# RWKV attention, Fourier mix and MLP on one core: weights requested later, masks from two-input VectorE operations, sums and state carry of two batches moved to VectorE, a new order

## The chip, the cores and the metric

The kernel runs on one core of a Trainium2 chip. Times are device microseconds (us), from launch to end; the span of a profile is from its first to its last instruction and is a little shorter. Five engines work side by side, each through its own list of instructions: TensorE (PE; its weight loads are shown as PEld), ScalarE (ACT), VectorE (DVE), GpSimd (POOL) and SyncE (SP), which issues most DMAs. They meet at semaphores.

## The reference

Inputs are r, k, v, w of 4 batches x 8 heads x 768 steps x 48, u of 8 x 48, and the two MLP weights. The attention is a recurrence over time, and its output goes through a Fourier mix, a normalization and an MLP:

```
state = 0
for t in range(S):
    cur = einsum('bhd,bhe->bhde', u * k[t], v[t])
    y[t] = einsum('bhd,bhde->bhe', r[t], state + cur)
    state = w[t][..., None] * state + einsum('bhd,bhe->bhde', k[t], v[t])
x = y as (batch, 768, 384)
u = x + real(fft(fft(x, axis=1), axis=2))
un = (u - mean(u)) / sqrt(var(u) + 1e-6)
out = u + relu(un @ w_ch1) @ w_ch2        # 384 -> 1536 -> 384
```

## The kernel before

**Attention.** Each batch is cut into 6 chunks of 128 steps; chunk n is step c = n mod 6 of batch n // 6 (24 chunks). The function attention does one: SP loads w, k, r, v (192 KB each, 7 buffers of each, L434). ACT takes ln of w (L586). PE forms two sums of it over time with two matmuls of 384 columns, one with the strict mask MSK (L588, "cumE") and one with the negated mask NLE (L592, "cumI"), in two PSUM banks, tce and tci, and the chunk's total beside the second (L599, "tot", or with one mask matmul more "totm", L603). ACT takes exp of both (L594; L609 and L611 in batch 0, or the one exp2 of L613 later). DVE multiplies r into the first (rh, L628); k is multiplied into the second by DVE in batch 0 (L632) and by POOL later (kh, L636). POOL forms r*k*u, DVE sums it (dc, L620), POOL scales v by it (vtd, L623). PE transposes rh and kh (L644, L650), ACT evicts both (rtb, ktb, L653, L655), PE forms the scores (amat, L663), DVE masks and evicts them in two halves (ah, L668). PE forms the chunk's state (L680), adding the old state with an identity matmul of 384 columns (L678); DVE scales it by the decay, in batch 0 with one operation (stm, L687), later with two halves (st, L694). PE forms y (L704, L708). The term of u and v is added in batch 0 by an fp32 matmul ("diag", L716, then ACT copies x, L720) and later by a DVE addition (x, L722). DVE and POOL fold x for the Fourier transform (fold_d, L737: columns of x plus and minus their mirror image, helper line L399).

**Mix and MLP.** The function mix does one batch: PE matmuls of the folded x with the cosine and sine tables CS and SS (L764, "mmh"), ACT evicts (hcs, L772), POOL reverses (hcr, L774), matmuls with DTM and DTP (L785, "mm2"), DVE adds x (uf, L787) and takes mean and variance (L791, L793: bn_stats, bn_aggr), ACT normalizes (un, L796), PE transposes (L802), ACT evicts (unt, L807). Then two halves of three blocks of 128 rows each: 12 m1 blocks of 3 matmuls with W1 (L826), whose relu is done by ACT (L835) or, for two of twelve, DVE (L831), and 3 m2 blocks of 12 matmuls with W2 (L845), which DVE scales and adds to u (osb, L850) and SP stores (L854).

**Start.** POOL makes index rows with iota; DVE makes four masks from them with tensor_scalar (masks, L457 to L460); DVE and ACT make a quarter of the tables with sine (tables, L484); DVE mirrors them (mirrors, L506); ACT copies halves of them with sign +1 and -1 (tables_end, L526); PE picks rows (L549) and ACT evicts them as DTM and DTP (L553, L555). POOL requests the weights (L560, L562) once the k load of chunk 5 has landed; the w load of chunk 7, and so all of SP's list behind it, waits for W1 (L436). Twenty warm-up steps of two matmuls (L887) are spread over the first part.

**Order.** Every operation has a number, in the order in which the program text creates it. The list ORDER, written out at the top, gives all 1511 of them in one sequence; each engine's list is its share of that sequence, in that order, and it never leaves it: an operation that waits holds up all behind it on its engine. BANKS gives the PSUM bank of each tile in turn. The function op derives who waits for whom from what each operation reads and writes, and arrange adds the waits for a bank's last users. Priorities such as KW and the ready0 of the warm-up steps have no effect on the chip except through ORDER.

Of the kernel before, what the change touches and what calls it, by code (L numbers as in the profile page):

```python
# [12 lines left out]
    70, 0, 3, 7, 8, 9, 6, 1, 11, 10, 2, 4, 71, 72, 46, 73, 42, 44, 45, 43, 41, 5, 12, 34,  # L13
    37, 74, 40, 19, 105, 25, 1491, 20, 26, 75, 106, 21, 13, 23, 32, 22, 14, 24, 27, 107, 1492, 15, 29, 28,
    17, 16, 108, 76, 84, 30, 18, 88, 1493, 137, 38, 85, 31, 138, 35, 36, 86, 1494, 109, 49, 139, 77, 50, 110,
    111, 33, 87, 112, 78, 79, 140, 81, 80, 113, 121, 1495, 116, 82, 89, 123, 114, 169, 141, 91, 39, 48, 115, 93,
    142, 170, 122, 117, 1496, 83, 144, 143, 90, 145, 124, 125, 171, 47, 92, 146, 148, 153, 98, 1497, 94, 99, 172, 155,
    120, 95, 118, 149, 51, 130, 97, 147, 201, 173, 1498, 154, 126, 119, 175, 177, 202, 131, 157, 174, 127, 96, 176, 156,
    203, 53, 1499, 129, 180, 152, 100, 101, 158, 128, 204, 54, 181, 162, 150, 102, 159, 185, 178, 233, 132, 151, 205, 182,
    1500, 184, 187, 163, 234, 206, 104, 133, 179, 189, 161, 183, 208, 271, 235, 186, 1501, 134, 207, 52, 212, 160, 209, 188,  # L20
    210, 236, 194, 217, 190, 164, 55, 1502, 213, 211, 216, 195, 429, 191, 237, 165, 218, 136, 193, 430, 1503, 166, 261, 219,
    192, 239, 238, 221, 431, 272, 103, 220, 240, 242, 214, 196, 241, 279, 432, 247, 197, 246, 135, 262, 222, 249, 167, 280,
    56, 58, 281, 248, 198, 226, 215, 251, 282, 250, 227, 433, 223, 168, 263, 252, 224, 264, 265, 200, 283, 273, 225, 253,
    243, 435, 255, 1504, 228, 199, 229, 59, 244, 266, 254, 64, 230, 245, 256, 231, 65, 257, 232, 57, 284, 60, 267, 258,
    434, 274, 66, 275, 259, 61, 436, 260, 285, 268, 63, 286, 287, 276, 269, 288, 289, 290, 62, 67, 270, 458, 277, 444,
    459, 439, 291, 293, 302, 460, 446, 68, 322, 461, 294, 69, 303, 440, 304, 448, 295, 1505, 305, 443, 340, 437, 278, 441,
    311, 312, 438, 313, 292, 306, 1506, 1507, 445, 314, 341, 1508, 307, 315, 308, 1509, 442, 296, 447, 309, 449, 331, 316, 297,
    332, 1510, 317, 450, 298, 299, 323, 451, 324, 453, 310, 318, 333, 325, 300, 319, 342, 455, 301, 334, 320, 363, 321, 343,
    351, 326, 364, 487, 353, 462, 454, 344, 352, 359, 488, 354, 327, 367, 345, 335, 328, 365, 452, 346, 489, 357, 468, 336,
    368, 456, 358, 373, 490, 457, 337, 469, 369, 374, 349, 355, 516, 360, 491, 470, 464, 466, 371, 467, 517, 471, 492, 356,  # L30
    361, 494, 474, 493, 518, 372, 375, 502, 366, 362, 380, 472, 497, 519, 501, 463, 495, 350, 338, 465, 551, 381, 498, 496,
    473, 376, 370, 552, 503, 339, 499, 475, 520, 347, 482, 477, 553, 522, 526, 524, 484, 505, 348, 476, 483, 525, 382, 554,
    500, 530, 329, 507, 377, 383, 586, 532, 330, 504, 478, 378, 390, 587, 527, 506, 479, 391, 400, 481, 555, 588, 396, 561,
    528, 557, 511, 480, 397, 589, 559, 565, 402, 562, 401, 560, 521, 783, 485, 403, 567, 392, 563, 523, 590, 394, 512, 784,
    531, 393, 529, 412, 395, 513, 533, 785, 413, 534, 595, 535, 508, 486, 569, 536, 379, 592, 510, 385, 596, 599, 509, 594,
    537, 384, 540, 571, 564, 597, 386, 787, 539, 786, 598, 556, 404, 538, 558, 812, 591, 601, 514, 405, 566, 543, 593, 813,
    541, 568, 793, 814, 544, 603, 570, 408, 515, 605, 789, 815, 546, 791, 600, 572, 409, 414, 573, 797, 841, 794, 816, 398,
    574, 818, 842, 406, 545, 399, 788, 549, 602, 407, 548, 542, 820, 843, 387, 790, 795, 822, 604, 798, 578, 844, 792, 419,
    388, 550, 826, 579, 575, 799, 870, 845, 410, 577, 606, 576, 411, 871, 581, 415, 608, 821, 847, 607, 849, 872, 828, 420,
    850, 625, 817, 873, 609, 547, 855, 584, 800, 819, 585, 610, 421, 802, 905, 580, 633, 634, 874, 635, 636, 611, 807, 416,  # L40
    906, 809, 583, 422, 801, 612, 876, 878, 907, 803, 808, 626, 617, 618, 627, 417, 836, 879, 614, 424, 827, 389, 884, 616,
    837, 628, 629, 804, 582, 908, 630, 909, 829, 613, 637, 615, 638, 631, 639, 640, 619, 838, 886, 641, 620, 940, 621, 831,
    622, 806, 911, 642, 913, 623, 643, 644, 830, 805, 632, 941, 846, 645, 888, 851, 647, 848, 656, 423, 665, 890, 648, 856,
    649, 666, 646, 832, 667, 942, 650, 810, 624, 657, 914, 658, 668, 425, 857, 919, 943, 651, 944, 426, 659, 880, 652, 1137,
    859, 669, 653, 694, 695, 660, 1138, 696, 861, 796, 676, 677, 670, 685, 661, 671, 427, 858, 418, 654, 921, 686, 662, 697,
    687, 672, 865, 811, 655, 428, 881, 663, 673, 698, 678, 833, 664, 679, 923, 860, 1139, 823, 713, 834, 674, 925, 721, 680,
    1140, 852, 675, 709, 714, 824, 1166, 722, 723, 882, 710, 915, 1167, 717, 853, 724, 725, 835, 718, 1168, 949, 711, 688, 726,
    715, 681, 712, 1169, 689, 854, 875, 682, 719, 716, 877, 1147, 727, 1195, 699, 690, 720, 885, 705, 700, 916, 728, 1196, 707,
    691, 701, 887, 708, 950, 862, 1197, 706, 692, 864, 839, 702, 734, 693, 1148, 867, 1141, 866, 739, 703, 863, 825, 953, 735,
    704, 951, 889, 883, 1198, 917, 868, 1224, 683, 840, 736, 1151, 1176, 1225, 869, 684, 1226, 910, 1149, 891, 1170, 1205, 766, 892,  # L50
    912, 740, 920, 1227, 1150, 729, 737, 952, 1259, 893, 894, 744, 895, 1177, 730, 738, 767, 745, 896, 758, 918, 1260, 756, 759,
    1234, 1178, 897, 757, 1261, 746, 1180, 898, 1206, 922, 747, 752, 1262, 924, 748, 899, 1294, 753, 926, 1179, 1207, 749, 741, 928,
    1295, 900, 946, 731, 742, 948, 1296, 927, 945, 955, 764, 947, 732, 929, 743, 1199, 1142, 903, 957, 765, 954, 902, 760, 1144,
    733, 901, 959, 956, 1235, 930, 1201, 932, 761, 931, 1297, 1203, 958, 754, 933, 904, 1209, 1143, 1152, 960, 1208, 1204, 1145, 755,
    971, 979, 762, 1228, 1236, 935, 1146, 750, 962, 763, 980, 1172, 751, 1174, 934, 1154, 1175, 1171, 768, 1153, 961, 1263, 1173, 769,
    1156, 936, 1182, 1181, 1155, 963, 1157, 770, 964, 1238, 939, 1184, 1161, 965, 1183, 1186, 972, 1158, 1211, 1162, 1185, 973, 1163, 773,
    1159, 968, 774, 1160, 966, 1187, 771, 1200, 1190, 1188, 1298, 772, 1164, 970, 775, 1202, 1165, 937, 1273, 987, 1191, 988, 989, 990,
    1237, 991, 1189, 981, 982, 983, 992, 984, 1230, 1232, 985, 938, 1193, 967, 993, 1233, 994, 969, 974, 995, 975, 776, 1307, 996,
    1265, 1240, 976, 1300, 1192, 997, 977, 998, 777, 1213, 1194, 1219, 999, 978, 1001, 1210, 1019, 1215, 1267, 1002, 1269, 1220, 1020, 1268,
    1021, 1221, 1003, 1242, 1022, 1302, 1248, 1270, 1244, 1004, 1229, 778, 1231, 1023, 1275, 1212, 1005, 1010, 1011, 1214, 1024, 1012, 1239, 779,  # L60
    1025, 1000, 1006, 1013, 1277, 1007, 986, 1241, 1271, 1030, 1309, 1279, 1031, 1014, 780, 1243, 1015, 1026, 1303, 1016, 1008, 781, 1048, 1049,
    1028, 1050, 1009, 1017, 782, 1272, 1216, 1051, 1027, 1039, 1217, 1040, 1018, 1032, 1304, 1245, 1029, 1218, 1071, 1059, 1247, 1072, 1073, 1305,
    1060, 1065, 1052, 1074, 1306, 1077, 1246, 1066, 1067, 1033, 1078, 1079, 1053, 1068, 1034, 1061, 1054, 1035, 1063, 1080, 1062, 1311, 1055, 1064,
    1075, 1313, 1069, 1076, 1041, 1088, 1056, 1070, 1036, 1042, 1081, 1043, 1037, 1093, 1038, 1082, 1089, 1044, 1057, 1045, 1094, 1058, 1046, 1095,
    1047, 1264, 1100, 1096, 1266, 1102, 1101, 1097, 1274, 1299, 1118, 1103, 1301, 1276, 1098, 1119, 1308, 1278, 1222, 1114, 1099, 1249, 1090, 1223,
    1115, 1250, 1251, 1091, 1283, 1106, 1252, 1092, 1284, 1280, 1254, 1107, 1285, 1112, 1281, 1310, 1113, 1110, 1258, 1282, 1312, 1083, 1253, 1111,
# [219 lines left out]
def bass_rwkv6_finch__then__fnet_fourier_mix_kernel(  # L286
# [11 lines left out]
    DM = H * D  # L298
# [585 lines left out]
    for i in range(NW):  # L884
        def warm(e):
            for x in range(2):
                ins = e.matmul(ps(tw)[:, 0:384], MSK[:, :], IDW[:, :])  # L887
# [33 lines left out]
```

## Time and profile before

| | |
|---|---|
| median of 5 runs | 203.4 us (200.49 to 205.51) |
| the profiled execution | 203.4 us, span 201.4 us |
| TensorE clock granted | 1.00 |
| MLP matmuls (m1, m2) | 576, 128 x 384 columns |
| DMA | 26.26 MB, loads of 192 KB land 3.8 to 4.0 us after issue (median) |
| SP waits for W1 | 7.6 us, once |

The page of a profile gives, for each engine, busy time and share, then the span in 40 equal slices (digits are tenths busy), the DMA queues, the chain of work that ended last, and the costliest groups. Further views used below: windows (busy time per engine in stretches), the chain in order of time, the timeline, and groups kept apart by shape. In a group's row, "x48 | 31.5, 682 | 4.0 <-PE" means 48 instructions, 31.5 us busy, 682 ns each, 4.0 us of idle time just ahead of them, ended by PE. Instructions of one engine overlap a little, so two in a row start closer together than one lasts.

### The profile page before, as it was taken

The page shows a single profiled execution, that of the slowest core. Times are in us where ns is not written, and L with a number is a line of the kernel's source. Part 1 is how long each engine was busy: PE and PEld are TensorE (multiplying, and loading weights), DVE is VectorE, ACT ScalarE, POOL GpSimd, SP SyncE. Part 2 cuts the span into 40 slices and gives each one's busy share as a digit, 9 for nine tenths or more (in the row PEclk, how much of TensorE's full clock was granted, in tenths as well). Part 3 has the DMA queues.
Part 4 walks back from the last instruction along what each step waited for, and adds up shares of the span by engine and source line. Part 5 has one row for each costly group of instructions (what it writes and reads, how often), then busy time and mean ns, then how long its engine had stood idle before and what let it go on. Part 6 is the DMA issues. An engine that isn't in the chain of part 4 may idle for free.

```text
span 201.4 us, 4633 instructions
## 1 busy us (share of the span) xinstructions
PE 185.7 (92%) x1765; PEld 116.4 (58%) x1765; DVE 154.5 (77%) x340; ACT 144.6 (72%) x332; POOL 119.2 (59%) x148
## 2 busy tenths in 40 slices
PE   2798986996999999999999989999999999999993
PEld 1155653644666676676675656776666566665661
DVE  7889999566846999989989799999557985913123
ACT  5979982667999988689994788598966304795500
POOL 5685892467099898799999889698101653000000
PEclk9999999999999999999999999999999999999999
DMA  5999899999799999997898990111001011200033
GB/s 120 211 206 199 168 184 200 184 184 208 143 211 182 235 203 178 212 213 188 171 180 169 219 238 5 39 42 39 3 0 58 26 39 39 80 1 0 0 108 130
DMA packets 105272, 26.26 MB, mean 130 GB/s; under 512 B 100257, under 2 KB 104866, under 8 KB 105250
## 3 DMA queue, kind: packets, MB, share of 16 engines
q1 hardware_dynamic: 103298, 23.60, 55.3%
q0 software_dynamic: 1952, 2.36, 6.9%
q8 instruction: 14, 0.23, 0.5%
q14 instruction: 8, 0.07, 0.1%
HBM read 23.59 MB, written 4.72 MB: 141 GB/s over the span
## 4 chain that ended last, share of the span: by engine, by line
PE 44%; DVE 19%; SPq 13%; DMA 11%; POOL 6%; ACT 3%; issue 3%; DVEq 0%; POOLq 0%
PE bank L826 15%; PE bank L845 14%; SPq L434 13%; DMA in_v<-in_v_dram 9%; DVE ah L668 4%; POOL rk L399 3%; PE bank L785 3%; DVE xf L399 3%; DVE osb L850 2%; DMA in_r<-in_r_dram 2%; DVE xa L399 2%; PE bank L764 2%; PE bank L663 2%; DVE x L722 2%; DVE st L694 2%
## 5 line engine op out<-in xcount | busy, mean ns | idle before, releaser
L826 PE MATMUL bank<-unt,w 128*128 128x384 bf16 x288 | 54.1, 326 | 0.5 <-ACT unt L807 0.5
L845 PE MATMUL bank<-w,ht 128*128 128x384 bf16 x288 | 54.1, 326 | 0.0
L835 ACT ACTIVATE ht<-bank 128x384 bf16<-128x384 f32 x80 | 37.7, 495 | 15.3 <-PE bank L826 15.1
L826 PEld LDWEIGHTS bank<-unt,w 128*128 128x128 bf16 x288 | 26.1, 97 | 16.8 <-issue 0.8
L845 PEld LDWEIGHTS bank<-w,ht 128*128 128x128 bf16 x288 | 26.6, 98 | 15.6 <-DVE ht L831 0.2
L668 DVE TENSOR_TENSOR ah<-bank,msk 128x512 bf16<-128x512 f32 x48 | 31.5, 682 | 4.0 <-PE bank L663 3.8
L399 POOL TENSOR_TENSOR vtd<-in_v,dc 128x384 f32<-128x384 f32 x24 | 19.9, 833 | 16.8 <-DVE dc L620 15.8
L399 POOL TENSOR_TENSOR rk<-in_r,in_k 128x384 f32<-128x384 f32 x24 | 24.5, 1025 | 4.6 <-DMA in_r<-in_r_dram 4.1
L850 DVE SCALAR_TENSOR_TENSOR osb<-bank,rstd,x 128x384 f32<-128x384 f32 x24 | 14.7, 612 | 14.2 <-PE bank L845 11.4
L399 POOL TENSOR_TENSOR rk<-rk,ub 128x384 f32<-128x384 f32 x24 | 24.2, 1015 | 0.9
L399 POOL TENSOR_TENSOR kh<-in_k,e 128x384 bf16<-128x384 f32 x18 | 19.0, 1058 | 3.8 <-ACT e L613 3.8
L655 ACT ACTIVATE ktb<-bank 128x512 bf16<-128x512 bf16 x24 | 14.5, 610 | 5.2 <-PE bank L650 5.2
L399 POOL TENSOR_TENSOR xd<-x 128x385 f32<-128x385 f32 x9 | 9.0, 1003 | 14.6 <-DVE x L722 14.6
L628 DVE TENSOR_TENSOR rh<-bank,in_r 128x384 bf16<-128x384 f32 x24 | 13.1, 550 | 5.7 <-ACT bank L594 4.2
L413 ACT ACTIVATE un<-x,agg 128x384 bf16<-128x384 f32 x24 | 14.0, 611 | 3.0 <-DVE agg L793 3.0
L787 DVE TENSOR_TENSOR x<-bank,x 128x384 f32<-128x384 f32 x24 | 12.8, 545 | 4.0 <-PE bank L785 3.8
L653 ACT ACTIVATE rtb<-bank 128x512 bf16<-128x512 bf16 x24 | 14.7, 611 | 1.5 <-PE bank L644 1.3
L831 DVE TENSOR_SCALAR ht<-bank 128x384 bf16<-128x384 f32 x16 | 8.7, 549 | 8.8 <-PE bank L826 8.8
L620 DVE TENSOR_REDUCE dc<-rk 128x8 f32<-128x384 f32 x24 | 12.8, 543 | 2.6 <-POOL rk L399 1.9
L887 PE MATMUL bank<-idw,msk 128*128 128x384 bf16 x40 | 11.1, 383 | 3.9 <-DVE idw L403 3.9
L413 ACT ACTIVATE lb<-in_w 128x384 bf16<-128x384 f32 x24 | 12.9, 540 | 2.4 <-PE bank L588 1.9
L413 ACT ACTIVATE vb<-in_v 128x384 bf16<-128x384 f32 x24 | 12.7, 536 | 2.0 <-DMA in_v<-in_v_dram 1.5
(119 smaller groups left out, 380.8 us busy)
## 6 DMA issues: line engine op xcount, KB each, us to landing
in_w<-in_w_dram SPq DMA_DIRECT2D x24, 192.0 KB, 3.8
in_k<-in_k_dram SPq DMA_DIRECT2D x24, 192.0 KB, 4.0
in_r<-in_r_dram SPq DMA_DIRECT2D x24, 192.0 KB, 3.9
in_v<-in_v_dram SPq DMA_DIRECT2D x24, 192.0 KB, 3.9
out_dram<-osb SPq DMA_DIRECT2D x24, 192.0 KB, 2.3
w<-in_moe_w_ch_dram POOLq DMA_DIRECT2D x2, 1152.0 KB, 13.6
ht<-in_u_dram SPq DMA_DIRECT2D x1, 1.5 KB
```

Of the source, the lines that this page charges most:

```text
L399: return shared(lambda e: e.tensor_tensor(out=o, in0=a, in1=b, op=f))
L413: return lambda e: e.activation(o, a, f, **kw)
L434: return e.dma_start(INB[n][i][:, :, :], src[n][b, :, c * CH:(c + 1) * CH, :].rearrange("h t d -> t h d"))
L620: op("dve", "dc", lambda e: e.tensor_reduce(out=dc[:, :], in_=rku[:, :, :], axis=mybir.AxisListType.X, op=ALU.add), r=[("RK", i2)], w=[("D ...
L628: op("dve", "rh", lambda e: e.tensor_tensor(out=rh[:, :, 0:D], in0=ps(tce)[:, 0:DM].rearrange("t (h d) -> t h d", d=D), in1=rt[:, :, :], o ...
L653: op("act", "ev512", lambda e: e.activation(rT[:, :, :].rearrange("p h t -> p (h t)"), psb(trr)[:, 0:512], ACTF.Copy), r=[trr], w=[("RTB", ...
L655: op("act", "ev512", lambda e: e.activation(kT[:, :, :].rearrange("p h t -> p (h t)"), psb(trk)[:, 0:512], ACTF.Copy), r=[trk], w=[("KTB", ...
L668: masked[n] = op("dve", "ah", lambda e, x=x: e.tensor_tensor(out=ah[:, x:H:2, :], in0=ps(ta[x])[:, :].rearrange("p (h t) -> p h t", t=128) ...
L826: ins = e.matmul(ps(t)[:, 0:384], W1[:, m, 128 * j:128 * j + 128], unt[:, m, :], start=(m == 0), stop=(m == NM - 1))
L835: op("act", "ev384", lambda e, j=j, t=t, ht=ht: e.activation(ht[:, j, :], ps(t)[:, 0:384], ACTF.Relu), r=[t], w=[("HT", q % 2, j)])
L845: ins = e.matmul(ps(t)[:, 0:DM], ht[:, j, 128 * x:128 * x + 128], W2[:, j, :], start=(j == 0), stop=(j == NJ - 1))
L850: op("dve", "osb", lambda e, kb=kb, t=t, o=o: e.scalar_tensor_tensor(out=o[:, :], in0=ps(t)[:, 0:DM], scalar=rstd[:, kb:kb + 1], in1=uf[:, ...
```

## The change

- The weight requests no longer wait for k of chunk 5 but for w of chunk 6. In POOL's new list W1 stands behind vtd of chunk 4, W2 behind kh of chunk 6.
- Masks and the small constant rows (MSK, NLE, IDF, IDW, NEGM, SGB, SGS, H5, CP) are made with scalar_tensor_tensor, whose second input is a column of constants KC; the negated identity NIDW is made with the masks. POOL's zero fills now wait for the tables (TG).
- The second and third table halves (UPE) are made by DVE with KC columns in place of ACT; CS and SS rows are one element longer.
- In batches 2 and 3 (chunks 12 to 23, TCD) the second sum isn't a matmul: DVE adds ln w to the first sum in PSUM ("tcd", into the E2 buffer in SBUF), and ACT takes exp of its negative ("expn"). The total stands in the first sum's bank (exp4), so a chunk uses one bank less.
- In the chunks of those batches that have a state before and after (13 to 16 and 19 to 22, SAD) PE doesn't add the old state; DVE does ("sadd", PSUM plus SBUF, into the fp32 buffer SA) and scales in one operation ("sams", two SBUF inputs) in place of the two st halves. Their total is of the kind totm.
- Chunk 5 gets its diagonal term from the DVE addition in place of diag and the ACT copy.
- Warm-up: 13 + 16 steps on a zero tile WZ, filled at the start, in place of 20 on the mask.
- ORDER (1530 operations now) and BANKS are new throughout. In the new lists the row picks and evictions of DTM and DTP stand among the first two or three chunks in place of after chunk 5, and y of chunk 6 stands before the first m1.

```diff
-            chain(op("sp", "load", f, r=["W1"] if b * NC + c == NC + 1 and n == "w" else (), w=[("in", n, i)],
-                     sem="in_%s%d" % (n, i)))
+            o = op("sp", "load", f, r=["W1"] if b * NC + c == NC + 1 and n == "w" else (), w=[("in", n, i)],
+                   sem="in_%s%d" % (n, i))
+            chain(o)
+            loads[b * NC + c, n] = o
...
-        op("dve", "fill1", fill(PM1[:, 0:1], 1.0), w=["PM1a"])
-        op("dve", "fill1", fill(PM1[:, 1:2], -1.0), w=["PM1b"])
+        op("dve", "fill384", fill(WZ[:, :], 0.0), w=["WZ"])
+        for i, x in enumerate((1.0, -1.0, 0.5, -1e4)):
+            op("dve", "fill1", fill(KC[:, i:i + 1], x), w=["KC%d" % i])
...
-        op("dve", "cmp384", ts(IDW[:, :], CI[:, :], 0.0, None, ALU.is_equal), r=["CI"], w=["IDB"])
+        op("dve", "cmps384", stt(IDW[:, :], CI[:, :], 0.0, KC[:, 0:1].to_broadcast([128, 384]), ALU.is_equal, ALU.mult), r=["CI", "KC0"], w=["IDB"])
+        op("dve", "cmps384", stt(NIDW[:, :], CI[:, :], 0.0, KC[:, 1:2].to_broadcast([128, 384]), ALU.is_equal, ALU.mult), r=["CI", "KC1"], w=["NIDW"])
...
-            op(e, kind, fill(o, 0.0), w=w)
+            op(e, kind, fill(o, 0.0), r=[("TG", q) for q in range(3)] if e == "pool" else (), w=w)
...
-        op("dve", "neg384", ts(NIDW[:, :], IDW[:, :], -1.0, None, ALU.mult), r=["IDB"], w=["NIDW"])
...
+    ws, WN = [], ((6, "w"), (6, "w"))
+
     def weights():
-        op("pool", "loadw", lambda e: e.dma_start(W1[:, :, :], moe_w_ch1.rearrange("(q p) n -> p q n", p=128)),
-           r=[("in", "k", 5)], w=["W1"], sem="w1")
...
+        ws.append(op("pool", "loadw", lambda e: e.dma_start(W1[:, :, :], moe_w_ch1.rearrange("(q p) n -> p q n", p=128)),
+           w=["W1"], sem="w1"))
...
-    KHD, DIAG, RKD = range(6), range(6), ()
-    FE, UPE, MST, HCD = ("act", "pool", "pool", "pool"), ("act", "act"), range(NC), ()
+    KHD, DIAG, RKD = range(6), range(5), ()
+    FE, UPE, MST, HCD = ("act", "pool", "pool", "pool"), ("dve", "dve"), range(NC), ()
+    TCD, SAD = range(12, 24), range(12, 24)
...
-        mst = n in MST
+        sad = n in SAD and not first
+        mst = n in MST or sad
+        tcd = n in TCD
...
-        tce, tci = g.tile(pool), g.tile(pool)
+        tce = g.tile(pool)
+        tci = tce if tcd else g.tile(pool)
...
-        if early:
+        if tcd:
+            op("dve", "tcd", lambda e: e.tensor_tensor(
+                out=e2[:, :, :], in0=ps(tce)[:, 0:DM].rearrange("t (h d) -> t h d", d=D), in1=L[:, :, 0:D], op=ALU.add),
+               r=[tce, ("LB", i2)], w=[("E2", i2)])
+            if not last:
+                op("act", "exp4", lambda e: e.activation(E2[i2][:, DM:ne], ps(tce)[:, DM:ne], ACTF.Exp), r=[tce], w=[("WE", i2)])
+            op("act", "exp", lambda e: e.activation(ps(tce)[:, 0:DM], ps(tce)[:, 0:DM], ACTF.Exp), w=[tce])
+            op("act", "expn", lambda e: e.activation(E2[i2][:, 0:DM], E2[i2][:, 0:DM], ACTF.Exp, scale=-1.0), w=[("E2", i2)])
+        elif early:
...
-                if not first:
+                if not first and not sad:
                     e.matmul(ps(tds)[:, 0:DM], IDB[:, :], s_in.rearrange("p h d -> p (h d)"), start=True, stop=False)
...
+            if sad:
+                op("dve", "sadd", lambda e: e.tensor_tensor(
+                    out=SA[:, :, :, :].rearrange("p h x d -> p (h x d)"), in0=ps(tds)[:, 0:DM],
+                    in1=s_in.rearrange("p h d -> p (h d)"), op=ALU.add),
+                   r=[tds, ("ST", (c + 1) % 2, 0), ("ST", (c + 1) % 2, 1)], w=["SA"])
             if mst:
-                op("dve", "stm", lambda e: e.tensor_tensor(
+                op("dve", "sams" if sad else "stm", (shared if sad else lambda f: f)(lambda e: e.tensor_tensor(
...
-    W0, WP, NW = 4.0, 1.6, 20
+    W0, WP, NW = 1.4, 0.65, 13
+    W1T, WP1, NW1 = 10.5, 1.6, 16
...
+    for o, n in zip(ws, WN):
+        o.deps.add(loads[n])
...
-                ins = e.matmul(ps(tw)[:, 0:384], MSK[:, :], IDW[:, :])
+                ins = e.matmul(ps(tw)[:, 0:384], WZ[:, 0:128], WZ[:, :])
```

## The prediction, made before the changed kernel was run

> **What bounds the kernel now.** I read the page first: shares of busy time, then the slices.
>
> ```profile
> span 201.4 us, 4633 instructions
> PE 185.7 (92%) x1765; PEld 116.4 (58%) x1765; DVE 154.5 (77%) x340; ACT 144.6 (72%) x332; POOL 119.2 (59%) x148
> ...
> DVE  7889999566846999989989799999557985913123
> ```
>
> TensorE (PE) leads, VectorE (DVE) is full in slices 14 to 28 and free at the end. Each engine works through its own list in ORDER, so counting a list off against the timeline names every instruction. Four stages follow: until the first m1 matmul of the MLP (50.0), until x of chunk 11 (83.1), until x of chunk 23 (163.1), the rest. The windows:
>
> ```profile
> 0.00:40.00 40.00, 30.89 (x297) 17.64 (x298) 34.96 (x81) 29.85 (x68) 25.57 (x37) 1.00 0.99 184
> 40.00:83.00 43.00, 41.09 (x425) 25.90 (x423) 33.28 (x71) 37.20 (x89) 32.40 (x37) 1.00 0.99 193
> 83.00:125.00 42.00, 40.86 (x425) 26.78 (x424) 38.33 (x83) 34.45 (x80) 39.38 (x45) 1.00 0.85 179
> 125.00:163.00 38.00, 37.74 (x391) 24.83 (x390) 31.74 (x71) 26.33 (x60) 18.14 (x24) 1.00 0.08 28
> 163.00:201.40 38.40, 35.15 (x236) 21.24 (x233) 16.16 (x37) 16.77 (x39) 3.73 (x6) 1.00 0.15 52
> ```
>
> Columns are PE, PEld, DVE, ACT, POOL, granted clock, DMA share, GB/s. A pipelined PE looks busy while it waits, so I count matmul work instead, by start-to-start times: 0.163 us for 384 columns (40 in 6.51 us in the chain), 0.083 for 192, 0.055 for 128. That gives 146.5 us of work between 50.0 and PE's end at 198.3: PE is full from the first m1 on. In the third stage DVE is busy 38.33 + 31.74 = 70.1 of 80.1 us, against 78.3 us of matmul work: the second limit is close behind. DMA is full until 121, when the last load lands, but x of chunk 17 comes at 124 while its loads landed at 92, so loads don't set the pace there.
>
> Before 50.0 it is different. The chain of waits:
>
> ```profile
> 27.20 17.30 DMA in_v<-in_v_dram
> 44.53 0.52 ACT vb L413
> 45.05 0.39 ACT e L613
> 45.51 1.00 POOL kh L399
> 46.56 0.41 PE bank L650 x4
> 47.00 0.60 ACT ktb L655
> 47.59 1.01 ACT un L413 x2
> 48.60 1.28 ACT unt L807 x3
> ```
>
> The v load of chunk 6 lies 17 us behind the weights (requested at 25.7 and 27.6); ScalarE (ACT) stands behind it in order, and un, which the first MLP needs, stands behind that. And the timeline of DVE shows one fold of 193 columns held up:
>
> ```profile
> 28.28 0.54 DVE L628 TENSOR_TENSOR rh<-bank,in_r 128x384 bf16<-128x384 f32 x1
> 28.74 3.33 DVE L399 TENSOR_TENSOR xf<-x 128x193 bf16<-128x193 f32 x2
> ...
> 32.11 0.54 DVE L632 TENSOR_TENSOR kh<-bank,in_k 128x384 bf16<-128x384 f32 x1
> ```
>
> Its fellows take 0.35. Kh of chunk 5 waits behind it.
>
> **What the skill says.** "SBUF — State Buffer", section "Who interferes with whom": a DVE instruction with two SBUF inputs contends with GpSimd (POOL) instructions that read SBUF, not with those that only write; a two-port tensor_scalar contends with both. The trace agrees: the fold above lasts from 28.74 to 31.8, through four POOL multiplies in a row, and the tensor_scalar tn<-tc takes 1.88 us beside POOL's memsets where one-column fellows take 0.14. "TensorE: Matmul & The Clock Gate", Part 1: a cold array takes N/1.2 ns, a warm one about half. Here the sum matmuls at 10.08, 10.40 and 10.72 start 0.32 apart, later ones 0.163: cold until about 13 us though the granted clock reads 1.00. "DMA: Bandwidth & Descriptors", "Issuing engines are not separate DMA queues": weights and loads share the same 16 engines; the 17.30 us landing agrees.
>
> **The change, stage by stage.** DVE costs below are start to start in the timeline: 0.47 us for 384 columns, 0.65 for a pair of st halves, 0.6 for an ah.
>
> *Stage 1 (to 50.0).* (a) Weights wait for the w load of chunk 6 (landed 28.2) and W2 stands in POOL's list behind kh of chunk 6, about 35. The k, r and v loads of chunk 6, issued by 27.2, then have only W1 beside them and should land by 32 instead of 44.5. Un of block 2 is ready at 46.2, when its bn_aggr is done, and ran at 47.5; un of block 0 was ready at 46.5 and ran at 48.0: 1.5 us off the path. SP's w load of chunk 7 still waits for W1, with all of SP's list behind it: W1 (10.5 us from request to landing now, sharing with four loads) lands by 37 to 40 against 36.2. In POOL's list W1 stands behind vtd of chunk 4 (done 29.5 now), when w of chunk 6 has landed, so rku of chunk 5 behind it loses the issue alone, 0.93. Hidden: chunk 7 isn't needed before 46. If the cover is gone, batch 1 starts up to 3 us late. (b) DVE until the last fold of batch 0 (ends 39.15): gone are the waits of tn (1.75 of its 1.88 us; POOL's memsets now wait for the tables, and the masks have two-input forms), negm (0.8 of 0.96), nidw (0.55 of 1.02), and the stall of 2.7, since list and POOL order are new: -5.8. Added: four table halves from ACT, which no row has on DVE; 576 elements by the price of "VectorE: DVE Perf Modes", the errata table, (58 + 576)/0.96 = 0.66, an estimate, against 0.45 for 288 in the row of ss<-ss,sgs, so 0.62 apart, 2.5 in all (0.45 each if two elements a cycle went through, 1.6 each if POOL stands in the way as it did for one mirt at 1.08); x of chunk 5 as an addition 0.47; rh and dc of chunk 6 moved ahead 0.94; memset 0.4: +4.3. Net -1.5. (c) Six table evictions of ACT (0.53 each) move from 37 to 42 up to the first chunks: 0.5 off the path; ACT gives up 2.9 of table halves there and takes 3.2. (d) Warm-up matmuls on zeros from 1.6 us: sums of the first chunks halve, about 1 us of PE that DVE's list hides. Diag of chunk 5: 0.64 us of PE, hidden too. Sum: first m1 at 50.0 - 1.5 - 1.5 - 0.5 = 46.5, **-3.5**.
>
> *Stage 2.* By the lists, PE has 29.7 us of work to y of chunk 11, against 32.1 (two sums with their totals, a y and two m2 blocks fewer; the y and the m2 are only moved): **-2.4**.
>
> *Stage 3.* PE loses 9 sum matmuls and 8 identity matmuls of the state (0.163 each, less 0.05 for the mask matmul that totm adds): -2.4; the new order brings 3.4 of MLP into the stage: 79.3 against 78.3. DVE gets 11 tcd and 8 sadd (PSUM input, 0.47 as rh), 8 sams (two SBUF inputs; 0.46 as xa unhindered, 0.70 as xa's mean) and gives up 16 st halves: 5.2 + 3.8 + 3.7 - 5.2 = 7.5, and 1.8 of other instructions move in: 70.1 + 9.3 = 79.4. ACT: exp2 (0.49) becomes exp4, exp, exp with exp4 0.06 start to start: nothing, hidden at 7.9 of 10. One PSUM bank less per chunk: gain not seen in any wait, I take nothing. SP's list puts two stores ahead of v of chunk 11 (issued 60.9); they need osb at 62.7 and 63.5, which moves ahead with the start: nothing. So both engines need 79.4 us. DVE's densest 30 us (70 to 100) are filled 28.8/30 = 0.96; 79.4/0.957 = 83: **+2.9**.
>
> *Stage 4.* 34.4 us of matmuls after y of chunk 23 against 36.0: **-1.6**; the tail of 3.1 us stays.
>
> Sum: 201.4 - 3.5 - 2.4 + 2.9 - 1.6 = 196.8 us of span; with the 2.0 that the profiled execution has around it (203.4, also the median of the five runs, 200.49 to 205.51) 198.8.
>
> **Rivals.** *DVE sets the end* (slower): every chunk of batches 2 and 3 passes tcd, sadd and sams one after the other, and sams waits for POOL, itself 0.92 busy from 70 to 120. For: DVE is on the chain at 75 to 97 and 113 to 123 already. Against: five slices after 140 have room. It decides when stage 3 exceeds 80.1 + 7.5 = 87.6 us, a DVE filled under 0.906. At its present 0.875 stage 3 takes 90.7: 206.5; at 0.86, as from 100 to 120, 208.1. *DVE fits in and PE is the limit*: 79.3 at PE's 0.987 (146.5 in 148.3) is 80.4, +0.3: 196.2. *The start gains nothing*: table halves and masks wait for POOL (1.6 each is +4) and eat the 3.5: 202.3. *Weights late*: W1 at 40 and batch 1 three us late: 201.8.
>
> **How the numbers follow.** My forecast 0.40 (own range 197 to 201), PE-limit 0.18, no start gain 0.16, DVE sets the end 0.20, weights late 0.06. Two per cent, about what a measurement of this kernel can tell from no change, are 199.3 and 207.5: faster is 0.18 + 0.24 of the forecast = 0.42; slower 0.14 of the DVE case and 0.01 elsewhere = 0.15; same 0.43. Range 195 to 207.
>
> **What would show it.** In the profile after: v of chunk 6 landing near 32 and no vb wait on in_v; the first m1 near 46.5; no xf fold above 1 us; cum matmuls 0.17 apart at 8 us; x of chunk 23 near 160, DVE filled 0.95 from 80 on. Wrong if m1 starts at 49 or later, if W1's landing ends a PE wait, or if DVE rows of sams average over 0.8 and x of chunk 23 comes after 164.

## The result, and the profile after

The changed kernel takes 202.7 us (median; 201.7 to 205.3), the kernel before, measured beside it, 203.6. The ratio is 1.002, 95% interval 1.000 to 1.004: no change. Executions of one kernel spread by some per cent, and the ratios leave out those well above its fastest. Its profiled execution took 202.2 us, span 200.3. The first lines of its page, and the windows at the same cuts as before (columns as there):

```profile
span 200.3 us, 4665 instructions
...
PE 187.7 (94%) x1769; PEld 116.0 (58%) x1769; DVE 164.9 (82%) x358; ACT 142.6 (71%) x337; POOL 121.7 (61%) x148
...
DVE  8999999987249999999999999999799996821232
```

```profile
0.00:40.00 40.00, 36.12 (x346) 20.36 (x346) 37.78 (x91) 30.10 (x70) 31.30 (x41) 1.00 0.93 174
40.00:83.00 43.00, 39.95 (x398) 24.97 (x395) 34.19 (x73) 33.07 (x80) 28.97 (x35) 1.00 1.05 202
83.00:125.00 42.00, 40.60 (x422) 26.11 (x420) 41.48 (x86) 34.79 (x86) 35.09 (x41) 1.00 0.85 180
125.00:163.00 38.00, 37.18 (x388) 24.14 (x387) 36.03 (x77) 28.25 (x66) 22.78 (x28) 1.00 0.09 33
163.00:200.30 37.30, 33.84 (x226) 20.38 (x224) 15.47 (x33) 16.43 (x39) 3.52 (x6) 1.00 0.13 48
```

VectorE is at nines from 60 to 165 us, but for a seven at 140: 41.48 of 42 in the third window, against 38.33 before. That looks like a VectorE-bound stage, and it mostly is not, as will be shown. Counting the lists off against the traces gives the four stages of the prediction. "Work" counts each matmul as the time to the next start, but no more than its columns need (0.16 us for 384); "idle" is the rest of TensorE's time, in stage 4 up to about its last matmul.

| stage | before: us, work, idle | after: us, work, idle | forecast | measured |
|---|---|---|---|---|
| 1, to the first m1 | 50.0 | 47.6 | -3.5 | -2.4 |
| 2, to x of chunk 11 | 33.1, 31.3, 1.9 | 31.9, 29.1, 3.0 | -2.4 | -1.2 |
| 3, to x of chunk 23 | 80.1, 73.5, 6.5 | 82.8, 73.6, 9.1 | +2.9 | +2.7 |
| 4, to the end | 38.3, 33.7, 1.1 | 37.9, 32.7, 1.6 | -1.6 | -0.4 |

From the first m1 on TensorE lost 3.1 us of work (138.5 to 135.4) and got 4.2 us of idle. One row of the list of TensorE's waits (in all, times, longest), before and after:

```profile
PE bank L764 <- DVE xf L399: 2.7, 2, 2.4
```

```profile
PE bank L789 <- DVE xf L402: 2.7, 5, 0.8
```

L764 and L789 are the Fourier matmuls, xf the folds. The sums are equal, but 2.4 us of the first fall into stage 1; in stage 3 alone the row reads 0.3 before and 1.5 after, and 0.4 and 2.3 when the gaps between matmul starts are counted. The timeline of VectorE after, and below it GpSimd's in the same stretch, at the last folds of batch 1:

```profile
79.49 1.43 DVE L402 TENSOR_TENSOR xf<-xa 128x193 bf16<-128x193 f32 x2
...
82.77 1.01 DVE L402 TENSOR_TENSOR xf<-xa 128x193 bf16<-128x193 f32 x1
83.70 1.15 DVE L402 TENSOR_TENSOR xf<-xd 128x193 bf16<-128x193 f32 x1
```

```profile
82.56 2.06 POOL L402 TENSOR_TENSOR kh<-in_k,e 128x384 bf16<-128x384 f32 x2
```

A fold of this shape takes 0.35 alone. Both here stand beside kh of chunks 12 and 13 on GpSimd and end 0.2 us after one of them does. Summing over stage 3 what each VectorE instruction took beyond the shortest of its kind gives 4.9 us before and 7.8 after; I call this hold-ups.

### The profile page after: what moved, and what is told of

Read it like the earlier page. It is cut to its first block, busy times and chain, and to the rows that moved or that the text cites. A ratio compares the mean times of both kernels' runs of the same rounds, so it can differ in the third digit from the quotient of the medians.

```text
span 200.3 us, 4665 instructions
## 1 busy us (share of the span) xinstructions
PE 187.7 (94%) x1769; PEld 116.0 (58%) x1769; DVE 164.9 (82%) x358; ACT 142.6 (71%) x337; POOL 121.7 (61%) x148
## 4 chain that ended last, share of the span: by engine, by line
PE 60%; DVE 29%; ACT 8%; issue 2%; DVEq 0%
PE bank L851 19%; PE bank L870 16%; DVE xf L402 6%; DVE ah L688 5%; PE bank L915 4%; PE bank L810 3%; PE bank L789 3%; DVE xa L402 2%; DVE osb L875 2%; PE bank L683 2%; DVE x L747 2%; PE bank L664 2%; DVE rh L648 2%; PE bank L827 2%; PE bank L670 1%
## 5 line engine op out<-in xcount | busy, mean ns | idle before, releaser
L688 DVE TENSOR_TENSOR ah<-bank,msk 128x512 bf16<-128x512 f32 x48 | 31.0, 678 | 0.3
L402 POOL TENSOR_TENSOR rk<-in_r,in_k 128x384 f32<-128x384 f32 x24 | 26.6, 1112 | 7.1 <-DMA in_r<-in_r_dram 6.9
L402 POOL TENSOR_TENSOR vtd<-in_v,dc 128x384 f32<-128x384 f32 x24 | 20.4, 852 | 3.0 <-DVE dc L640 2.7
L402 POOL TENSOR_TENSOR kh<-in_k,e 128x384 bf16<-128x384 f32 x18 | 18.4, 1020 | 5.0 <-ACT e L633 3.0
L416 ACT ACTIVATE un<-x,agg 128x384 bf16<-128x384 f32 x24 | 14.6, 627 | 5.3 <-DVE agg L818 5.3
L915 PE MATMUL bank<-wz 128*128 128x384 bf16 x58 | 15.6, 392 | 1.4 <-DVE kc L413 1.4
L402 POOL TENSOR_TENSOR xd<-x 128x385 f32<-128x385 f32 x9 | 9.5, 1052 | 11.3 <-DVE x L747 11.0
L789 PE MATMUL bank<-cs,xf 128*128 128x193 bf16 (+2 forms) x48 | 10.3, 269 | 3.4 <-DVE xf L402 2.7
```

The costliest lines, as they stand in the source:

```text
L402: return shared(lambda e: e.tensor_tensor(out=o, in0=a, in1=b, op=f))
L416: return lambda e: e.activation(o, a, f, **kw)
L688: masked[n] = op("dve", "ah", lambda e, x=x: e.tensor_tensor(out=ah[:, x:H:2, :], in0=ps(ta[x])[:, :].rearrange("p (h t) -> p h t", t=128) ...
L789: return e.matmul(ps(t)[:, k0:k1], xf[:, f, off:off + 128], tab[:, s, k0:k1], start=a, stop=z, skip_group_check=True)
L915: ins = e.matmul(ps(tw)[:, 0:384], WZ[:, 0:128], WZ[:, :])
```

## The experiments

Three theories. V: VectorE's time sets stage 3, as the prediction had it. P: TensorE's list and its own waits set it, and VectorE's work is covered. Q, formed after the first runs: the hold-ups of two-input VectorE instructions beside GpSimd's cost what the matmuls saved. Ratios are to the kernel before, measured beside each run. In some of the profiles (table halves on ScalarE, only the folds freed, thirteen waits, ten waits with shortened additions, the changed kernel with other banks) a stretch of 3.41 us at the first m1 ran at a granted clock of 0.50: there the m1 matmuls start 0.32 us apart in place of 0.16, and stage 2 reads 1.5 to 1.7 us longer, so it is not compared. The profile with only the folds freed has a second such stretch in stage 3.

**1. Parts undone, and VectorE's additions shortened.** What stays keeps its order on each engine; the operations of the old kind take their places in ORDER (with the old carry, the state matmuls of chunks 14 and 15 move five places back on TensorE), and BANKS changes with them. The second diff shows the outputs alone.

```diff
-    TCD, SAD = range(12, 24), range(12, 24)
+    TCD, SAD = range(12, 24), ()             # e1; e2: (), range(12, 24); e3: (), ()
```

> The changed kernel with the state carry back on TensorE (no sadd, no sams; st halves, identity matmul and tot as in the kernel before), all else as changed. VectorE gives up 8 x (0.47 + 0.47 - 0.65) = 2.3 us in the third stage (x of chunk 11 to x of chunk 23), TensorE gets 8 x 0.11 = 0.9 us. Theory V, VectorE sets the third stage (82.8 us, filled 0.97): 1 to 2 us faster than the changed kernel, that is 0.5 to 1% under the kernel before. Rival P, TensorE's list sets it and the additions are hidden: 0.5 to 1 us slower than the changed kernel, 0.5% over the kernel before.

> The changed kernel with the second sum back as a matmul in its own bank and one exp2 (no tcd, no expn), all else as changed. VectorE gives up 12 x 0.47 = 5.6 us, TensorE gets 12 x 0.163 = 2.0 us. Theory V: 2 to 3.5 us faster than the changed kernel, 1 to 1.5% under the kernel before. Rival P: 1.5 to 2 us slower than the changed kernel, about 1% over the kernel before. Third case, the second bank was what mattered: slower by more than 2 us, with new waits of matmuls for banks.

> The changed kernel with both moves to VectorE undone: it keeps the later weights, the masks, the table halves, the warm-up and the new order. VectorE gives up 7.9 us, TensorE gets 2.9 us. Theory V: third stage back to 79 or 80 us, 2.5 to 4 us faster than the changed kernel, 1.2 to 1.8% under the kernel before. Rival P: 2 to 3 us slower than the changed kernel.

```diff
-  tcd: out=e2[:, :, :]    sadd: out=SA[:, :, :, :]    sams: out=s_out[:, :, :]
+  tcd: out=e2[:, 0:1, :]  sadd: out=SA[:, 0:1, :, :]  sams: out=s_out[:, 0:1, :]   # inputs cut to match
```

> The changed kernel, order and waits untouched, with tcd on 48, sadd and sams on 96 of their 384 columns, so that the rest of the decay and of the state is left out: VectorE loses about 12 x 0.35 + 16 x 0.3 = 9 us of work, TensorE nothing. Theory V: 2.5 to 5 us faster than the changed kernel, 1 to 2.3% under the kernel before. Rival P: within 0.5 us of the changed kernel.

| | ratio, interval | stage 3 | its work, idle | VectorE busy |
|---|---|---|---|---|
| changed kernel | 1.002 | 82.8 | 73.6, 9.1 | 80.4 |
| state carry on TensorE | 1.036 (1.033 to 1.040) | 89.2 | 74.7, 14.3 | 79.1 |
| second sum on TensorE | 1.015 (1.011 to 1.019) | 84.7 | 75.5, 9.2 | 76.1 |
| both | 1.038 (1.034 to 1.043) | 89.9 | 76.6, 13.3 | 74.1 |
| additions shortened | 1.004 (1.001 to 1.006) | 82.3 | 73.7, 8.6 | 75.9 |

With less on VectorE the stage was never shorter by more than 0.5. The second sum on TensorE adds the 1.9 us of its matmuls and nothing else. The old state carry costs 6.4 us, which no theory gave; experiment 6 comes back to it. But the shortened run was no clean test: one sams of 96 columns lasted 3.6 us beside four GpSimd instructions in a row, hold-ups rose from 7.8 to 10.6, and TensorE waited 1.9 us behind it. That gave theory Q.

**2. The state on PSUM, so that sams has one SBUF input; and the same shortened.** BANKS had to change too.

```diff
-  sadd: out=SA, in0=ps(tds)      sams: in0=SA
+  sadd: out=ps(tds), in0=ps(tds) sams: in0=ps(tds)
```

> The changed kernel, but sadd writes its sum back into its PSUM bank and sams reads it there, so that sams no longer has two SBUF inputs; nothing else differs. In the changed kernel the eight sams of stage 3 last 1.2 us longer together than eight of the shortest. Theory Q (what costs in stage 3 is VectorE instructions with two SBUF inputs held up beside GpSimd's): sams all last 0.54, stage 3 falls from 82.8 by 0.5 to 1.2. Theory P (TensorE's list and its own waits): 82.8 within 0.3. A PSUM bank held 0.6 us longer could cost: above 83.3. Stages 1, 2 and 4 as in the changed kernel (47 to 48.5, 31.9, 37.9).

> The kernel with shortened additions (tcd on 48, sadd and sams on 96 columns, the rest of the decay sums and of the state left out), now with sadd and sams on PSUM as well. There the sams of 96 columns were held up for 4.3 us together, one for 3.6, so that the shortening had taken away only 1.5 us of VectorE in all, and the test of VectorE's load was not clean. Theory V (VectorE's time sets stage 3): with the hold-ups gone as well, VectorE needs about 73 us in stage 3, which falls from 82.3 to 79.5 or below. Theory P: 82 within 0.5. Theory Q: sams clear, the folds still held up as in that kernel (2.2 us): 80.5 to 81.5.

Stage 3: 86.4 and 84.2; ratios 1.023 (1.018 to 1.027) and 1.009 (1.006 to 1.013). Sams all lasted 0.52 to 0.56, but TensorE now stood at bank reuse (transposes and m1 matmuls waiting for ht of ScalarE, 1.5 us, and more). The first expectation named this cost as possible, not its size; experiment 6 comes back to it.

**3. The start.** Table halves back on ScalarE; SP's gate one chunk later; six warm-up steps less.

```diff
-    FE, UPE, ... = ("act", "pool", "pool", "pool"), ("dve", "dve"), ...
+    FE, UPE, ... = ("act", "pool", "pool", "pool"), ("act", "act"), ...
...
-            ... r=["W1"] if b * NC + c == NC + 1 and n == "w" else () ...
+            ... r=["W1"] if b * NC + c == NC + 2 and n == "w" else () ...
...
-    W0, WP, NW = 1.4, 0.65, 13
+    W0, WP, NW = 1.4, 0.65, 7
```

> The changed kernel with the four table halves back on ScalarE, at the same places of the sequence. On VectorE they last 3.0 us together before the last fold of batch 0 (39.4). If VectorE's list sets the start: last fold at 36.5 to 37, first m1 at 45 to 45.5 (47.6 now). If something else does (the recurrence through all engines, ScalarE): last fold within 0.7 of 39.4. ScalarE gets 2.9 us between 8 and 25 us, where it is about 0.8 busy: if it is the limit there, the last fold comes later than 39.4. Stages 2 to 4 as in the changed kernel.

> The changed kernel, but the load that waits for W1 is w of chunk 8 in place of w of chunk 7: SP is not held from 28 to 38, and chunk 7 (0.77 MB, about 4 us of all DMA) comes ahead, beside W1. The rival of late weights says that stage 2 lost half of its gain to in_r of chunk 7 (landed 48.6, GpSimd waits 6 us for it): then stage 2 falls from 31.9 to 31 or less. Otherwise 31.9 within 0.2: GpSimd's wait is covered. W1 would land at 41 to 43 (38.2 now), W2 at about 50 (46.7): a first m1 later than 48.5 would show that W1 is what it waits for.

> The changed kernel without six of its early warm-up steps (4 to 9, ahead of the first sum on TensorE's list, which they hold from 8.0 to 9.4). If the early warm-up costs the start: first sum at 8.1, rh of chunk 0 up to 1 us earlier, last fold of batch 0 and first m1 0.5 to 1.4 us earlier. If VectorE's list hides it (rh stands behind a table half that ends at 10.3): within 0.3; later, if the sums of chunks 0 and 1 run cold (0.32 a matmul in place of 0.16) and something waits for them.

Table halves on ScalarE: last fold 41.4, first m1 49.7, ratio 1.017 (1.012 to 1.023). VectorE lost 3.0 us of work but waited as long for exp of ScalarE (rh 1.7, kh 1.3), so that it was level again at 30 us, and then one fold was held up for 2.97 in place of 0.99: later, where the simple sum says earlier. Up to there ScalarE was the limit, the last case of the expectation. Gate: W1 landed at 37.5, W2 at 47.6, stage 2 31.9 as in the changed kernel, ratio 1.005 (1.003 to 1.007): GpSimd's 6 us of waiting for in_r was covered, so late weights are out. Warm-up: first m1 47.4, ratio 1.007 (1.005 to 1.009): VectorE's list hides it. Seven kernels here have the same stage 1 as the changed one and put the first m1 at 47.2 to 48.7. Much of this goes with the instant at which TensorE reaches its full rate: in the two at 47.2 its matmuls of 384 columns start 0.16 us apart from 5.0 us on, in the other five from 9.4 to 11.4 us on, and 0.32 apart until then.

**4. The folds freed, then every hold-up.** No list is changed; GpSimd gets waits.

```diff
+            if n in (12, 19):                                          # f3: kh
+                o.deps.add(folds[(n - 1) // 6 - (n == 19), 5])         # and vtd of chunk 6
...
+    for o, x in ((213, 104), (244, 168), (233, 259), (795, 545), (612, 582),
+                 (800, 615), (1183, 840), (1156, 900), (940, 939), (1189, 974)):
+        g.ops[o].deps.add(g.ops[x])                                    # g1: ten pairs
     g.arrange(ORDER, BANKS)
```

> The changed kernel with three waits added on GpSimd: kh of chunk 12 waits for the last fold of chunk 11, kh of chunk 19 for that of chunk 17, vtd of chunk 6 for the last fold of batch 0. The lists are the same. In the changed kernel these folds (xf of 193 columns on VectorE) last 1.01, 1.15, 1.18, 0.74 and 0.99 us against 0.35 alone, and the Fourier matmuls wait for them 0.60, 0.65, 0.77 and 0.24 us in stage 3. Theory Q: the folds take 0.35, fold waits of TensorE in stage 3 fall from 2.4 to below 0.6, stage 3 from 82.8 to about 81; stage 1 by 0.6. Theory P: other waits take their place (kh is 1 us later): stage 3 within 0.4 of 82.8. Slower than 83.2 if kh is what TensorE needs next.

With the three waits TensorE waited for no fold of stage 3 by more than 0.2 us any more, and stage 3 read 84.6, ratio 1.006 (1.002 to 1.009). Of the 84.6, at most 1.7 come from the second stretch at half clock:

```profile
108.43:111.84 3.41, 3.40 (x26) 2.38 (x26) 2.44 (x6) 2.06 (x6) 2.11 (x2) 0.50 0.50 114
```

Without it the stage is at 82.9 or a little more, no shorter than 82.8, though its fold waits of 2.3 us are gone. The hold-up had moved. VectorE, then GpSimd, of this kernel:

```profile
102.62 4.03 DVE L717 TENSOR_TENSOR st<-sa,e 128x384 bf16<-128x384 f32 x1
```

```profile
102.55 0.99 POOL L402 TENSOR_TENSOR rk<-in_r,in_k 128x384 f32<-128x384 f32 x1
103.50 0.99 POOL L402 TENSOR_TENSOR kh<-in_k,e 128x384 bf16<-128x384 f32 x1
104.46 0.82 POOL L402 TENSOR_TENSOR vtd<-in_v,dc 128x384 f32<-128x384 f32 x1
105.25 0.98 POOL L402 TENSOR_TENSOR rk<-rk,ub 128x384 f32<-128x384 f32 x1
```

This sams needs 0.54. It began 0.07 after rk and ended 0.4 after the fourth GpSimd instruction; ah stood behind it, and TensorE waited 2.3 us for that. So all of them had to be freed at once:

> The changed kernel with ten waits added on GpSimd, and no list changed: wherever a two-input VectorE instruction was held up by 0.4 us or more, the GpSimd instruction that it met waits until it is done (rk of chunk 4 for the fold of chunk 0, rku 5 for fold 2, xfo 4 for fold 5, rku 12 for xa 9, xd 11 for fold 10, kh 12 for the folds of 11, rk 19 for sams 13, vtd 18 for sams 15, xd 16 for xa 16, kh 19 for the folds of 17). Freeing only the folds had moved the hold-up to sams of chunk 13 (3.5 us), and stage 3 did not fall. Theory Q (stage 3's lost time is these hold-ups, wherever they stand): hold-ups of VectorE in stage 3 from 7.8 to about 4, TensorE's waits for folds from 2.4 to under 0.6 and none over 1 us for ah, stage 3 from 82.8 to 80 to 81; stage 1 one to two us shorter (the folds of batch 0 lose 2.4); span near 197. Theory P (the list's own waits; GpSimd is late instead): stage 3 within 0.5 of 82.8. Slower if GpSimd, held back ten times by 0.3 to 1 us, becomes what the lists wait for.

Ratio 0.980 (0.975 to 0.985), median 197.6 us, span 195.9: faster than both kernels. Stage 1 46.0, stage 2 31.2, stage 3 80.8; hold-ups in stage 3 4.1. The groups of VectorE kept apart by shape, of the changed kernel and of this one (count, busy us, mean ns):

```profile
L402 DVE TENSOR_TENSOR xf<-xa 128x193 bf16<-128x193 f32 x9 | 6.1, 685 | 0.1
L402 DVE TENSOR_TENSOR xf<-x 128x193 bf16<-128x193 f32 x6 | 5.7, 991 | 0.0
```

```profile
L402 DVE TENSOR_TENSOR xf<-xa 128x193 bf16<-128x193 f32 x9 | 4.5, 507 | 0.1
L402 DVE TENSOR_TENSOR xf<-x 128x193 bf16<-128x193 f32 x6 | 1.9, 356 | 0.0
```

In the changed kernel the six folds of batch 0 alone lose 3.8 us, and they stand on the path to the first m1. Three waits more:

```diff
-                 (800, 615), (1183, 840), (1156, 900), (940, 939), (1189, 974)):
+                 (800, 615), (1183, 840), (1156, 900), (940, 939), (1189, 974),
+                 (1213, 870), (942, 941), (150, 56)):
```

> The kernel with ten waits on GpSimd, and three more for what was still held up there: rk of chunk 20 waits for sams of chunk 14 (1.18 us in place of 0.54), xfo of chunk 16 for xfe of chunk 16 (0.75), rku of chunk 2 for the table half CS1 (1.08 in place of 0.74). Theory Q: up to 0.6 us less in stage 3 (80.8 with ten) and 0.3 in stage 1, if TensorE waits for these; nothing if it doesn't, as its waits for VectorE in stage 3 are down to 1.2 us. Slower if a hold-up comes up elsewhere.

Ratio 0.980 (0.976 to 0.985), stage 3 79.3. Only the fold came free: sams of chunk 14 still took 1.18, the half 0.91. The ratio shows no gain, but four of its six executions had a mean granted clock of 0.991, as the profile has with its stretch at half clock, so it can't tell.

**5. What is left of V, and the kernel before with such waits.**

> The kernel with ten waits on GpSimd, with the additions shortened (tcd on 48, sadd and sams on 96 columns; the rest of the decay sums and of the state left out): VectorE's own work with the hold-ups out of the way. Theory V (VectorE's time sets stage 3): it loses 4.5 to 5.5 us of work there, stage 3 falls from 80.8 towards TensorE's 73.6 of work and 6 of small gaps, to 79.5 or below. Theory P with Q (the hold-ups were the cost, VectorE's plain work is hidden): 80.8 within 0.5.

Ratio 0.977 (0.973 to 0.980), stage 3 79.8. The two windows that hold stage 3, with ten waits and with ten waits and shortened additions:

```profile
77.22:158.02 80.80, 78.94 (x829) 51.90 (x828) 76.81 (x167) 63.88 (x154) 59.15 (x70) 1.00 0.55 123
```

```profile
77.33:157.08 79.75, 78.16 (x830) 52.20 (x828) 69.48 (x167) 63.50 (x153) 58.65 (x71) 1.00 0.56 125
```

VectorE gives up 7.3 us and the stage 1.0, to 79.8: between what V (79.5 or below) and P with Q (80.8 within 0.5) gave. Each of the two stages holds one wait of TensorE at the Fourier matmuls, here in the same order:

```profile
PE bank L810 <- ACT rtb L673: 1.1, 1, 1.1
```

```profile
PE bank L810 <- ACT rtb L673: 1.6, 1, 1.6
```

Behind it is a load: w of chunk 16 landed at 85.3 and 85.7, ScalarE waited for it 1.5 and 2.2 us, and rtb stands behind it in ScalarE's list. With thirteen waits this load landed at 82.2 and there is no such wait; that, more than its three waits, makes 79.3. Less these waits the stages are 79.7 with ten waits, 78.2 with shortened additions, 79.3 with thirteen. So 7.3 us of VectorE's work are worth 1.0 to 1.5 us: V as the main price falls, the added work is covered for the most part at 0.96 busy, and with the hold-ups gone the loads begin to count.

```diff
+    for o, x in ((116, 50), (149, 47), (215, 135), (585, 584), (1206, 899),
+                 (902, 903), (1235, 901), (1153, 934)):
+        g.ops[o].deps.add(g.ops[x])                                    # in the kernel before
     g.arrange(ORDER, BANKS)
```

> The kernel before with eight waits of the same sort on GpSimd, at the places where its VectorE was held up: rk 1 for a mirrored half of SS, rku 2 for one of CS, vtd 4 for fold 1 (3.06 us), xfo 10 for fold 10, rku 20 for xa 15, xfo 15 and rku 21 for the folds of 15, kh 18 for xa 16. If its start is set by in_v of chunk 6 (landed 44.5) and not by VectorE, the last fold of batch 0 comes 2 us earlier and the first m1 stays at 50 within 0.4; in stage 3 TensorE waits for folds 0.4 us only: 80.1 within 0.6. Then the waits on GpSimd are worth 0 to 0.5% there, and 1.8% on the changed kernel. If they are worth 3 us here too, the gain is no part of what the change opened.

Ratio 0.994 (0.990 to 0.997). The fold of 3.06 us takes 0.35, the last fold comes at 36.3 (39.2 before), and the first m1 stays at 50.3. Stage 3 is 79.3, 0.8 shorter, a little more than expected. The chain of waits says why the start stays:

```profile
26.21 18.61 DMA in_v<-in_v_dram
...
44.85 0.52 ACT vb L413
...
48.92 1.28 ACT unt L807 x3
```

In this profile the load sets the start, and hold-ups there are free; the change took the load off and left the hold-ups to set it. The profiled execution took 202.6 us and the shortest of this kernel 198.5, so it is not shown that the load sets the start in every execution.

**6. Banks.** Other PSUM banks for the same lists: for the changed kernel, for the state on PSUM, for the state carry on TensorE, and for both parts undone with ten waits. Only BANKS differs from the runs above (and, in the last, waits are added).

> The changed kernel with other PSUM banks for the same lists: each tile gets a bank that by the trace of the changed kernel was free for 0.6 us or else longest; openings of a tile less than 0.25 us after the bank's last use fall from 77 to 24. Theory B (waits for banks hold TensorE: holding one bank 0.5 us longer in eight chunks cost 3.6 us of stage 3): stage 3 falls by 1 us or more, stage 2 by 0.5. Otherwise both within 0.4 of 82.8 and 31.9: then the banks are tight but just enough.

> The changed kernel with sadd and sams on PSUM, as in the first of these runs (stage 3 at 86.4), with banks chosen by the trace so that tiles opened less than 0.25 us after the bank's last use fall from 102 to 59. If the 3.6 us came from a poor choice of banks: stage 3 at 83 to 83.5. If they come from eight banks being too few when one is held longer (all are taken at 92 to 98): 85.5 or more. Stages 1, 2, 4 as in the changed kernel.

> The changed kernel with the state carried by TensorE again (identity matmul, two st halves, total of its old kind), as in the first of these runs (stage 3 at 89.2, ratio 1.036), with banks chosen by the trace. The same choice of banks took 3.3 us off stage 3 where sadd and sams work on PSUM. If the loss of 6.4 us was mostly banks: stage 3 at 84.5 to 86. If it was the state chain (each state matmul waits for the st of the chunk before): 88 or more. TensorE has 1.1 us more work in the stage either way.

> The changed kernel with ten waits on GpSimd (those of the thirteen that are not on sams), with both the decay sums and the state carry back on TensorE, and banks chosen by the trace. Thirteen waits with both on VectorE gave stage 3 of 79.3 and ratio 0.980. If moving the sums and the carry is worth what TensorE loses of work (3.0 us): stage 3 at 82 to 83. If the start alone carries the gain: 79 to 80.5. Above 84 if the old state chain does not suit the new lists.

| | ratio, interval | stage 3 (with the first banks) |
|---|---|---|
| changed kernel | 1.000 (0.997 to 1.003) | 82.7 (82.8) |
| state on PSUM | 1.006 (1.003 to 1.009) | 83.1 (86.4) |
| state carry on TensorE | 1.012 (1.006 to 1.019) | 85.7 (89.2) |
| both undone, ten waits | 1.008 (1.006 to 1.011) | 86.0 |

So 3.3 to 3.5 us of two earlier losses were my choice of banks, and the first reading of the state carry (6.4 us) is corrected to 2.9, of which 1.1 is work. In the last run stage 1 is as short as with the waits (44.6), and stage 3 is 86.0 with 76.7 of work and 9.4 of idle, against 73.6 and 5.6 with both parts on VectorE and thirteen waits. The moved sums and carry are worth their 3.1 us of matmuls; how much of the other 3.6 is the old chain and how much lists and banks that were made for the new one stays open.

## Why the prediction was wrong, step by step

- **Forecast and outcome.** 198.8 us was 0.977 of the kernel before; it came out at 1.002. Of the 3.5 us by which the span missed (200.3 for 196.8), stages 1, 2 and 4 have 1.1 to 1.2 each. With GpSimd waiting at ten places the same change stands at 0.980: stages 1 to 3 get back 1.6, 0.7 and 2.0 us in the profile, stage 4 nothing. So what was missed in stages 1 to 3 is mainly the hold-ups. Of the signs listed, "no xf fold above 1 us" failed seven times (1.01 to 1.53); none of the signs of being wrong came.
- **TensorE was not full.** The 146.5 us of matmul work that the forecast counted come to 138.5 by the count above, with 9.5 idle. In stages 2 and 4 the forecast took matmuls off the time one for one and put new idle at nothing; 1.1 and 0.5 came.
- **Stage 1, the failed step: "the stall of 2.7, since list and POOL order are new: -5.8".** The other three terms of that sum came true (tn 0.16, negm 0.16 and less, nidw 0.54), and the four table halves took 0.75 each, 0.66 estimated. But the new order did not remove the hold-ups, it dealt them anew: the six folds lost 3.8 us to them (2.96 before), and the last fold ended at 39.37 where 37.65 was forecast. Freed, it ended at 35.9 to 37.4 and the first m1 came at 44.5 to 46.0, which the forecast had at 46.5. Among kernels whose TensorE reached full rate at the same instant, the waits bring the first m1 from 47.2 to 44.5 (5.0 us) and from 48.7 to 46.0 (11.4 us).
- **Stage 1, the weights: right.** v of chunk 6 landed at 31.87 (32 forecast), W1 at 38.2, and the 1.5 us of un came off the path (un of block 2 was ready at 45.8 before, not 46.2, which changes nothing). The w load of chunk 7 landed 2 us later than before and cost nothing, as the gate run shows: "weights late" is out.
- **Stage 2: half right.** Matmul work fell by 2.2 (2.4 forecast). Idle rose by 1.1: TensorE waited 0.4 for an ah and 0.2 for an x on VectorE, which stood behind xa of chunk 9 (1.35 in place of 0.54). With it freed both waits are gone and stage 2 is 31.2.
- **Stage 3: the right number by luck.** "Both engines need 79.4 us" made VectorE's density the price. VectorE's work is covered for the most part (7.3 us are worth 1.0 to 1.5); the matmul work grew by 0.1, where I had +1.0 (my 78.3 and 79.3 held the small gaps too); and the whole 2.6 is idle, about 2 of it the Fourier matmuls waiting for folds. I counted the two-input sams at 0.46, as if unhindered (between starts; they last 0.54 alone and lasted 0.68 in the mean), and did not ask what the folds would meet.
- **Stage 4: -1.6 forecast, -0.4.** Work fell by 1.0, so 0.6 was mis-sized; idle rose by 0.5. Two folds of chunk 23 were held up too (1.05 and 0.77, 0.35 alone), but no run frees them, so it stays open what they cost.
- **Rivals.** "DVE sets the end" named the waiting of sams for GpSimd, the right mechanism, but as load over a whole stage; its test fell. "PE is the limit" had 80.4 for stage 3, near the 80.8 with ten waits; its total, 0.965 of the kernel before, is not reached (0.980). "The start gains nothing" had hold-ups in it, for table halves and masks, where they were small; they hit the folds.
- **The skill.** "SBUF — State Buffer", section "Who interferes with whom", says which pairs contend: a VectorE instruction with two SBUF inputs and a GpSimd one that reads SBUF. The trace agrees: each of the changed kernel's hold-ups of more than 0.2 us is such a pair (5.4 of the 7.8 us in stage 3; the rest is small scatter). What it costs is decided by the instant, and no sum over rows shows it.

## What to carry to other kernels

When a new order is made for VectorE and GpSimd, list the two-input VectorE instructions on the path and what GpSimd runs at that instant; a wait on GpSimd's side (covered here at ten places) keeps the pair apart, while the new order here only moved the meetings. Free all of them before judging, since freeing one may only let the next be hit. And before a full engine is called the bound, shorten its work with the hold-ups gone: here 7 of 77 us brought 1.0 to 1.5. Before stages are compared, look for stretches at a lower granted clock, window by window.

## What the runs showed of the hardware that was not expected

- One VectorE instruction can be held through four GpSimd instructions in a row (4.03 us for 0.54; 3.63 for a sams of 96 columns), another of the same form gets in after one (1.24 and 0.94). What decides was not found.
- The added VectorE instructions last 0.54 us at 384 columns, 0.25 at 96 and 0.20 at 48. By these three, an estimate, about 0.15 us is fixed and 1.0 ns comes with each column.
- Holding one PSUM bank about 0.5 us longer in eight chunks cost 3.6 us with one choice of banks and 0.3 to 0.5 with another, on the same lists.
- Stretches of 3.41 us at a granted clock of 0.50, with matmuls of 384 columns 0.32 us apart, come in some executions and cost up to 1.7 us each. What sets them off is not shown.
- The record of the granted clock begins only near the first matmuls at full rate: at 14.2 us before and 9.3 after, where these first start 0.16 us apart at 15.2 and 9.4. So 1.00 in the window from 0 says nothing of the slow part ahead of it, and the forecast was wrong to set it beside that part.
